# A job's scores, and its products of decayed scores and values, as single operations of a planner

## The chip, the cores and the metric

The kernel runs on one core of one Trainium2 chip. The time is device microseconds from start to end of an execution; the figure of a kernel is the median of its runs.

## What is computed

The reference is a gated linear-attention layer followed by two feed-forward layers, all in float32:

```
for t in range(768):                                  # 4 batches, 8 heads, head size 40
    m_new  = max(f_gate[t] + m, i_gate[t])
    f_stab = exp(f_gate[t] + m - m_new); i_stab = exp(i_gate[t] - m_new); m = m_new
    C = f_stab * C + i_stab * outer(v[t], k[t])
    n = f_stab * n + i_stab * k[t]
    y[t] = sigmoid(o_gate[t]) * (C @ q[t]) / max(abs(n . q[t]), 1)
x = y as 3072 tokens of 320
x = (h - tanh(h)) @ w_out,  h = x @ w_in              # 320 -> 2048 -> 320
x = g(h) @ w_out,  h = x @ w_in,  g(h) = h for h >= 1, 0 for h <= -1, (h + 1)^2 / 4 between
```

## The kernel before

The attention is done in chunks of 128 positions. A *job* is one chunk of one batch with its 8 heads; there are 24 jobs, numbered by chunk first and batch second. In a job the scores of each head (keys times queries, 128 by 128) are multiplied by a matrix of decays, and the product is multiplied with the values of the chunk. The earlier chunks enter through a state C that each job hands on to the next job of its batch.

On TensorE a job consists of these groups of matmuls, in the order of their priorities: the scores (`score`, line 465 in the profile; 8 matmuls, two at a time on two halves of the rows of the array, into two PSUM banks `t_s`), the products with the old state (line 503), the products of decayed scores and values (`pv`, line 509; 16 matmuls, two at a time on two halves of the columns of the array, into the bank `t_n`), the transposes of the result (line 532, `t_x`), and the new state (line 539, `t_c`). Each float32 matmul stands in the trace as two instructions, so a job has 16 of line 465 and 32 of line 509. VectorE makes the decays by a scan (line 453, tile `d`, a buffer for each half of the heads, three buffers in rotation) and multiplies the scores into them (line 471). Behind the products stand, in this order, ACT line 519 (the denominators, `dn`), VectorE lines 520 and 521, GpSimd line 522, VectorE line 526 (`x`), ACT line 529, and the transposes. The bank `t_n` is a single buffer. After the first two chunks the transposes of the gates (line 369, `t_i`; four of the six) use that same buffer.

The feed-forward layers run over 6 blocks of 512 tokens and 16 slices of 128 hidden units each, that is 96 steps per layer. A step has 8 matmuls for h (line 612; line 604 in the first steps) and 8 for the output (line 655; 12 in the second layer). The jobs of a block run during the feed-forward steps of the block before; the jobs of the first block run before any feed-forward step. In the first layer the weights are also converted on ACT and VectorE (lines 315 to 330).

The order on every engine is fixed ahead of time by a planner (`Plan`). Each operation has an engine, a cost in ns, a priority, and the buffers it reads and writes. On each engine the planner picks, among the operations that can start within 150 ns of the earliest one, that with the lowest priority number; ties go to the earlier start, then to the order in which they were stated. It counts 170 ns after a TensorE operation plus 60 ns until another engine may use the result, and 130 ns from another engine to TensorE. The instructions are then issued in that order, and each engine runs its own in order. Until the first feed-forward step the planner puts matmuls on zeros (line 755, `spare`) into the gaps that it foresees on TensorE.

Line 444 (`t_f`) spreads the decays of the first four jobs over the partitions by matmuls, and line 568 copies their transposed results for the first feed-forward steps.

Of the kernel before, what the change touches and what calls it, by code (L numbers as in the profile page):

```python
# [17 lines left out]
B, H, S, D = 4, 8, 768, 40  # L18
L = 128
# [5 lines left out]
E1 = D + 1  # L25
G3 = 3 * E1
HU = H // 2
# [45 lines left out]
class Plan:  # L73
# [20 lines left out]
    def op(self, eng, ns, prio, fn, r=(), w=(), out=None, lock=False):  # L94
        o = Op()
        o.eng, o.ns, o.prio, o.fn, o.seq, o.out = eng, ns, prio, fn, len(self.ops), out
        o.allocs, o.preds, o.succs = [], set(), []
        o.bufs, o.fill, o.lock = [], 0, lock
        key = lambda x: x if isinstance(x, tuple) else (x, None)

        for x in map(key, r):
            if x in self.last:
                o.preds.add(self.last[x])
            self.read.setdefault(x, []).append(o)
        for x in map(key, w):
            if x in self.last:
                o.preds.add(self.last[x])
            o.preds.update(self.read.pop(x, ()))
            self.last[x] = o
        o.preds.discard(o)  # L110
        for b in {key(x)[0] for x in (*r, *w)}:
            if isinstance(b, Buf):
                b.users.append(o)
                o.bufs.append(b)
        if any(b.place[0].startswith("late_") for b in o.bufs):
            o.preds.add(self.gate)
        self.ops.append(o)
        return o
# [102 lines left out]
def pe(n, m=128, wide=1):  # L221

    return max(wide * n / 2.4 + 13.5, m / 1.2 + 5)
# [3 lines left out]
def mlstm_moe_moe(ctx: ExitStack, tc: tile.TileContext, ig, fg, qk, q3, nat, w1, w2, cst, out):  # L227
    nc = tc.nc
# [25 lines left out]
    op = P.op  # L254
# [7 lines left out]
    def abuf(tag, shape, dtype, cap, name=None):  # L262
        att_tags.add(tag)
        return P.buf(of(ap), shape, dtype, tag, name or tag, cap)
# [128 lines left out]
    def jbank(n, what, name):  # L393

        tag = {"s0": "ta", "s1": "tb", "n": "tn", "x": "ta", "c": "tb", "f": "h"}[what]
        if n < FIRST and what in "s0s1xc":
            tag = (("ta", "tb"), ("a0", "a1"))[n % 2][what in ("s1", "x")]
        return bank(tag, name)
# [5 lines left out]
    def job(n, at, ld):  # L404

        c, b = divmod(n, B)
        last = c == NC - 1

        qt = abuf("qkraw", [64 + D, 1024], F32, 3)
# [25 lines left out]
        dk = {}  # L435
        d0 = wbuf(6 + n % 2, [128, 1024], F32, "d0") if n < FIRST else None
        wc = abuf("wc", [128, H], F32, 2)
        for u in range(2):
            p = at(0) if u == 0 else at(1)
# [8 lines left out]
            if d0 is None:  # L448
                d = abuf("d", [128, 512], F32, 3)
# [9 lines left out]

        sp = [jbank(n, f"s{u}", "t_s") for u in range(2)]  # L460

        def score(h):
            for u in range(2):
                t = qt[u * 64:u * 64 + D]
                nc.tensor.matmul(sp[u][:, h * L:(h + 1) * L], t[:, 512 + h * L:512 + (h + 1) * L],  # L465
                                 t[:, h * L:(h + 1) * L], start=True, stop=True)

        for h in range(HU):
            op("PE", 2 * pe(L, 128, 2), at(1), lambda h=h: score(h), [(qt, 0), (qt, 1)], [sp[0], sp[1]])
        for u in range(2):  # L470
            op("DVE", dve(512), at(2 + u), lambda p=sp[u], d=dk[u][0]: nc.vector.tensor_tensor(  # L471
                out=d(), in0=p.t, in1=d(), op=ALU.mult), [sp[u], dk[u][1]], [dk[u][1]])
# [2 lines left out]
        K, V, O = (nt, 0), (nt, 1), (nt, 2)  # L475
        v3 = lambda: nt[:, DM:DM + H * E1]
# [21 lines left out]
        p = jbank(n, "n", "t_n")  # L498
        parts = [(k, 120 if k < 2 else 80, G3 if k < 2 else 2 * E1) for k in range(3)]
        if c > 0:  # L500
            C = Cst[b, c]
            for k, r, w in parts:
                op("PE", 2 * pe(w, 128, 2), at(2.5), lambda k=k, r=r, w=w: nc.tensor.matmul(  # L503
                    p[:, k * G3:k * G3 + w], q[0:r, k, :], C[0:r, k * G3:k * G3 + w],
                    start=(k == 0), stop=False, skip_group_check=True), [(q, k // 2), C], [p])
        def pv(d, h):

            for z in (0, 64):
                nc.tensor.matmul(  # L509
                    p[z:z + 64, h * E1:(h + 1) * E1], d[:, z:z + 64], v3()[:, h * E1:(h + 1) * E1],  # L510
                    start=(c == 0 and h == 0), stop=(h == H - 1), skip_group_check=True)

        for u in range(2):
            for i in range(HU):
                h = u * HU + i
                op("PE", 125, at(4), lambda u=u, i=i, h=h: pv(dk[u][0]()[:, i * L:(i + 1) * L], h), [dk[u][1], V], [p])
        pn = lambda: p[:, 0:H * E1].rearrange("p (h e) -> p h e", e=E1)
        dn = abuf("dn", [128, H], F32, 1)
        op("ACT", 180, at(5), lambda: nc.scalar.activation(dn.t, pn()[:, :, D], AF.Abs), [p], [dn])
# [16 lines left out]
        if not last:  # L536
            pc = jbank(n, "c", "t_c")
            for k, r, w in parts:
                op("PE", 2 * pe(w, 120, 2), at(7), lambda k=k, r=r, w=w: nc.tensor.matmul(  # L539
                    pc[0:r, k * G3:k * G3 + w], nt[:, k * 120:k * 120 + r], v3()[:, k * G3:k * G3 + w],  # L540
                    start=True, stop=True), [K, V], [pc])
# [4 lines left out]
            for h in range(3):  # L546
                op("ACT", 330, at(8), lambda h=h: nc.scalar.activation(
                    y(to, h), y(pc, h), AF.Copy, scale=cs[0:120, C_HM + h:C_HM + h + 1]), [pc, "cs"], [to])
                if h < 2:
                    z = slice(2 * G3 + h * E1, 2 * G3 + (h + 1) * E1)  # L550
                    op("ACT", 280, at(8), lambda h=h, z=z: nc.scalar.activation(
                        to[0:80, z], pc[0:80, z], AF.Copy, scale=cs[0:80, C_HM + h:C_HM + h + 1]), [pc, "cs"], [to])
            if old is not None:
                for k, r, w in parts:
                    z = slice(k * G3, k * G3 + w)
# [10 lines left out]
        z = slice((n - BLK0[k]) * L, (n - BLK0[k] + 1) * L)  # L566
# [200 lines left out]
    def jobs(k):  # L767
        for i, (a, _) in enumerate(GROUPS):
            if i > 1 and a * B == BLK0[k]:
                gates(i, GATES[i])  # L770
                decays(i, DECAYS[i])
        for n in range(BLK0[k], BLK0[k] + BLK[k]):
            if k == 0:
                job(n, lambda s: JOB0 + JOBD * n + JOBS * s, LOAD[n])
            else:
                st = NF * (k - 1) + NF * (n - BLK0[k]) / BLK[k] - AHEAD
                job(n, lambda s: st + s, st - LOADS)
# [5 lines left out]
    for f in range(NF):  # L783
        p = W_CONV[f] if f < len(W_CONV) else f - W_AHEAD
# [102 lines left out]
```

## Time and profile before

| | us |
|---|---|
| median of 3 runs | 849.0 |
| lowest and highest run | 844.51 and 849.15 |
| the profiled execution | 847.22 |
| its span, first to last instruction | 845.4 |
| TensorE busy in the span | 831.9 |
| VectorE, ACT, GpSimd busy | 562.7, 417.0, 134.1 |

The profile shows one execution. The span leaves out 1.8 us that lie around it. A matmul's shown duration reaches beyond the start of the next one, since they overlap; what a group costs TensorE is read from its start to the start of the next row.

### The profile page before, as it was taken

To read this page: it belongs to the slowest core of one execution; us is meant where nothing else is said; L and a number is where in the kernel's file an instruction comes from. 1 tells how busy PE (TensorE), PEld (TensorE's weight loads), DVE (VectorE), ACT (ScalarE), POOL (GpSimd) and SP (SyncE) were. 2 spreads that over 40 slices of the span, in tenths; PEclk is the share of its full clock that TensorE was granted. 3 is DMA by queue.
4 is the path that set the end of the run, shared out by engine and by line. 5 is a ranking of instruction groups with operands and counts; after the bars stand their busy time and mean duration, and the time that the engine had idled before them with its cause. 6 is when DMAs were issued, how large, how long until landed. Compare 5 with 4: busy or idle time off the path is not lost.

```text
span 845.4 us, 13194 instructions
## 1 busy us (share of the span) xinstructions
PE 831.9 (98%) x5027; PEld 691.4 (82%) x5031; DVE 562.7 (67%) x920; ACT 417.0 (49%) x792; POOL 134.1 (16%) x170
## 2 busy tenths in 40 slices
PE   8999998999999999999999999999999999999997
PEld 6647766787888788878888889999999999999997
DVE  6998998888878756565446675565555655655554
ACT  3877755666665534433345553443443433433432
POOL 3231124322223321121003020020100100100000
PEclk9999999999999999999999999999999999999999
DMA  8974557566765432341145320020010000000000
GB/s 220 349 219 141 180 185 246 171 214 223 239 196 171 120 107 90 84 140 39 37 147 158 103 88 1 1 82 1 16 66 0 32 2 1 32 1 1 32 1 31
DMA packets 56515, 88.02 MB, mean 104 GB/s; under 512 B 4708, under 2 KB 37892, under 8 KB 56452
## 3 DMA queue, kind: packets, MB, share of 16 engines
q1 hardware_dynamic: 56404, 87.17, 32.8%
q8 instruction: 39, 0.64, 0.3%
q14 instruction: 24, 0.20, 0.1%
q10 hardware_dynamic: 48, 0.02, 0.0%
HBM read 72.59 MB, written 14.58 MB: 103 GB/s over the span
## 4 chain that ended last, share of the span: by engine, by line
PE 84%; DMA 0%; issue 0%; DVE 0%; DVEq 0%
PE h L612 39%; PE a L655 32%; PE t_o L655 5%; PE t_n L509 2%; PE t_s L465 2%; PE t_n L503 1%; PE t_c L539 1%; PE t_x L532 1%; DMA fb<-fr_d 0%; DVE C L556 0%; PE t_i L369 0%; DVE ob L700 0%; DVE x L526 0%; DVE d L453 0%; DVEq L453 0%
## 5 line engine op out<-in xcount | busy, mean ns | idle before, releaser
L612 PE MATMUL h<-x,w 128*128 128x512 f32 x1504 | 388.9, 397 | 1.9 <-ACT w L326 1.5
L612 PEld LDWEIGHTS h<-x,w 128*128 128x128 f32 x1504 | 275.1, 188 | 57.2 <-ACT w L326 2.8
L643 DVE TENSOR_TENSOR gl<-g,gh 128x512 fp32r<-128x512 f32 x188 | 134.1, 713 | 94.6 <-ACT gh L642 93.5
L642 ACT CAST gh<-g 128x512 fp32r<-128x512 f32 x188 | 116.6, 620 | 117.9 <-DVE g L639 72.8
L655 PE MATMUL a<-gh,w 128*128 128x512 f32 x460 | 150.8, 395 | 0.3 <-ACT gh L642 0.3
L637 ACT ACTIVATE g<-g,half 128x512 f32<-128x512 f32 x96 | 69.4, 723 | 121.1 <-DVE g L635 121.1
L655 PE MATMUL a<-w,gh 128*128 128x320 f32 x576 | 127.7, 308 | 0.0
L639 DVE TENSOR_TENSOR g<-h,g 128x512 f32<-128x512 f32 x96 | 66.3, 691 | 75.5 <-ACT g L637 75.5
L655 PE MATMUL a<-gl,w 128*128 128x512 f32 x276 | 107.1, 393 | 0.0
L655 PEld LDWEIGHTS a<-w,gh 128*128 128x128 f32 x576 | 100.2, 188 | 7.3
L630 ACT ACTIVATE g<-h 128x512 f32<-128x512 f32 x92 | 54.9, 597 | 92.7 <-PE h L612 92.5
L655 PEld LDWEIGHTS a<-gh,w 128*128 128x128 f32 x460 | 85.2, 188 | 18.2 <-ACT gh L642 0.8
L631 DVE TENSOR_TENSOR g<-h,g 128x512 f32<-128x512 f32 x92 | 63.2, 687 | 54.9 <-ACT g L630 54.1
L655 PE MATMUL a<-w,gl 128*128 128x320 f32 x288 | 88.9, 309 | 0.0
L635 DVE TENSOR_SCALAR g<-h 128x512 f32<-128x512 f32 x96 | 66.2, 690 | 8.0 <-PE h L612 8.0
L655 PEld LDWEIGHTS a<-gl,w 128*128 128x128 f32 x276 | 51.6, 188 | 11.1 <-DVE gl L643 0.2
L655 PEld LDWEIGHTS a<-w,gl 128*128 128x128 f32 x288 | 54.0, 188 | 0.0
L583 POOL TENSOR_TENSOR x<-xl,x 128x1024 fp32r<-128x1024 f32 x6 | 14.5, 2412 | 241.1 <-ACT x L582 241.1
L453 DVE TENSOR_TENSOR_SCAN d<-fb,scan_id 128x512 f32<-128x512 f32 x40 | 49.4, 1239 | 4.1 <-PE t_n L509 3.4
L522 POOL TENSOR_TENSOR nat<-nat,dn 128x320 f32<-128x320 f32 x24 | 29.1, 1213 | 99.3 <-DVE dn L521 96.7
L655 PE MATMUL t_o<-w,gh 128*128 128x320 f32 x192 | 43.9, 309 | 0.0
L471 DVE TENSOR_TENSOR d<-t_s,d 128x512 f32<-128x512 f32 x48 | 31.2, 680 | 10.9 <-PE t_s L465 9.1
(105 smaller groups left out, 825.2 us busy)
## 6 DMA issues: line engine op xcount, KB each, us to landing
w<-in_w_dram SPq DMA_DIRECT2D x32, 703.6 KB
nat<-in_nat_dram SPq DMA_DIRECT2D x24, 484.0 KB
fb<-fr_d SPq DMA_DIRECT2D x40, 256.0 KB
qkraw<-in_qk_dram SPq DMA_DIRECT2D x48, 160.0 KB
w_d<-w SPq DMA_DIRECT2D x16, 352.0 KB
w<-w_d SPq DMA_DIRECT2D x16, 352.0 KB
xr_d<-xo SPq DMA_DIRECT2D x18, 256.0 KB
q<-in_q_dram SPq DMA_DIRECT2D x20, 180.0 KB
```

What stands on the lines that cost most here:

```text
L453: op("DVE", dve(1024), p, lambda o=dk[u][0], i=f[u][0]: nc.vector.tensor_tensor_scan(out=o(), data0=i(), data1=scan_id, initial=0.0, op0=A ...
L471: op("DVE", dve(512), at(2 + u), lambda p=sp[u], d=dk[u][0]: nc.vector.tensor_tensor(out=d(), in0=p.t, in1=d(), op=ALU.mult), [sp[u], dk[u ...
L522: op("POOL", pool(DM), at(5), lambda: nc.gpsimd.tensor_tensor(out=o3().rearrange("p (h e) -> p h e", e=D), in0=o3().rearrange("p (h e) -> ...
L612: op("PE", pe(n), prio, lambda i=i, c=c, s=s: nc.tensor.matmul(p[:, :n], w[:, c:c + 128], x[:, s, :n], start=(i == 0), stop=(i == 7)), [(w ...
L630: op("ACT", act(n), prio + 0.5 - FFN, lambda: nc.scalar.activation(t[:, :n], p[:, :n], AF.Tanh), [p], [t])
L631: op("DVE", dve(n), prio + 0.5 - FFN, lambda: nc.vector.tensor_tensor(out=t[:, :n], in0=p[:, :n], in1=t[:, :n], op=ALU.subtract), [p, t], [t])
L635: op("DVE", dve(n), prio + 0.5 - FFN, lambda: nc.vector.tensor_scalar(t[:, :n], p[:, :n], -1.0, 1.0, op0=ALU.max, op1=ALU.min), [p], [t])
L637: op("ACT", act(n, 1), prio + 0.5 - FFN, lambda: nc.scalar.activation(t[:, :n], t[:, :n], AF.Square, bias=half[:, 0:1], scale=0.5), [t, "h ...
L639: op("DVE", dve(n), prio + 0.5 - FFN, lambda: nc.vector.tensor_tensor(out=t[:, :n], in0=p[:, :n], in1=t[:, :n], op=ALU.max), [p, t], [t])
L642: op("ACT", act(n), prio + 1 - FFN, lambda: nc.scalar.copy(gh[:, :n], t[:, :n]), [t], [gh])
L643: low = lambda e: e.tensor_tensor(out=gl[:, :n], in0=t[:, :n], in1=gh[:, :n].bitcast(F32), op=ALU.subtract)
L655: mm = lambda o, a, b, start, stop, r, cost: op("PE", cost, prio, lambda: nc.tensor.matmul(o(), a(), b(), start=start, stop=stop), r[0], r[1])
```

## The change

The four operations for a job's scores become one operation with the same eight matmuls in the same order, and its planned cost goes from 4 times 240 ns to 1088 ns. The eight operations for a job's products of decayed scores and values (one for each head, each depending on the decays of its own half of the heads) become one operation with the same sixteen matmuls in the same order; it depends on both halves, and its planned cost goes from 8 times 125 ns to 1128 ns.

```diff
-        def score(h):
-            for u in range(2):
-                t = qt[u * 64:u * 64 + D]
-                nc.tensor.matmul(sp[u][:, h * L:(h + 1) * L], t[:, 512 + h * L:512 + (h + 1) * L],
-                                 t[:, h * L:(h + 1) * L], start=True, stop=True)
-
-        for h in range(HU):
-            op("PE", 2 * pe(L, 128, 2), at(1), lambda h=h: score(h), [(qt, 0), (qt, 1)], [sp[0], sp[1]])
+        def scores():
+            for h in range(HU):
+                for u in range(2):
+                    t = qt[u * 64:u * 64 + D]
+                    nc.tensor.matmul(sp[u][:, h * L:(h + 1) * L], t[:, 512 + h * L:512 + (h + 1) * L],
+                                     t[:, h * L:(h + 1) * L], start=True, stop=True)
+
+
+        op("PE", 200 + 2 * HU * 111, at(1), scores, [(qt, 0), (qt, 1)], [sp[0], sp[1]])
...
-        def pv(d, h):
-
-            for z in (0, 64):
-                nc.tensor.matmul(
-                    p[z:z + 64, h * E1:(h + 1) * E1], d[:, z:z + 64], v3()[:, h * E1:(h + 1) * E1],
-                    start=(c == 0 and h == 0), stop=(h == H - 1), skip_group_check=True)
-
-        for u in range(2):
-            for i in range(HU):
-                h = u * HU + i
-                op("PE", 125, at(4), lambda u=u, i=i, h=h: pv(dk[u][0]()[:, i * L:(i + 1) * L], h), [dk[u][1], V], [p])
+        def pv():
+
+            for h in range(H):
+                d = dk[h // HU][0]()
+                for z in (0, 64):
+                    t = h % HU * L + z
+                    nc.tensor.matmul(
+                        p[z:z + 64, h * E1:(h + 1) * E1], d[:, t:t + 64], v3()[:, h * E1:(h + 1) * E1],
+                        start=(c == 0 and h == 0), stop=(h == H - 1), skip_group_check=True)
+
+        op("PE", 200 + 2 * H * 58, at(4), pv, [dk[0][1], dk[1][1], V], [p])
```

## Rows read from the trace of the kernel before

**Rows 1.** The page, parts 1 and 2: busy time of the engines, granted clock in tenths.
```profile
PE 831.9 (98%) x5027; PEld 691.4 (82%) x5031; DVE 562.7 (67%) x920; ACT 417.0 (49%) x792; POOL 134.1 (16%) x170
PEclk9999999999999999999999999999999999999999
```

**Rows 2.** Windows: stretch, its length, busy us per engine, clock, DMA share, GB/s.
```profile
41.00:128.60 87.60, 84.54 (x489) 57.39 (x489) 79.69 (x134) 61.01 (x118) 20.14 (x32) 1.00 0.59 181
...
131.60:135.60 4.00, 3.99 (x16) 2.95 (x16) 3.32 (x6) 1.30 (x4) 2.01 (x2) 0.57 0.68 233
135.60:380.00 244.40, 244.18 (x1639) 196.94 (x1640) 179.86 (x314) 132.87 (x296) 62.27 (x86) 1.00 0.52 166
```

**Rows 3.** Groups of TensorE instructions by line: count, busy us, mean ns, idle before.
```profile
L509 PE MATMUL t_n<-nat,d 128*64 128x41 f32 x768 | 31.1, 233 | 0.2 <-issue 0.2
```

**Rows 4.** Timeline of TensorE, job 20: start us, us, engine, line, instruction, count.
```profile
362.58 1.43 PE L612 MATMUL h<-x,w 128*128 128x512 f32 x5
363.94 0.67 PE L509 MATMUL t_n<-nat,d 128*64 128x41 f32 x16
364.53 0.50 PE L612 MATMUL h<-x,w 128*128 128x512 f32 x1
364.97 0.67 PE L509 MATMUL t_n<-nat,d 128*64 128x41 f32 x16
365.56 0.73 PE L612 MATMUL h<-x,w 128*128 128x512 f32 x2
366.14 0.62 PE L655 MATMUL a<-gh,w 128*128 128x512 f32 x2
```

**Rows 5.** Timeline of TensorE, job 21, from its scores on.
```profile
377.85 1.16 PE L465 MATMUL t_s<-qkraw 40*128 40x128 f32 x16
378.94 0.73 PE L612 MATMUL h<-x,w 128*128 128x512 f32 x2
379.51 0.62 PE L655 MATMUL a<-gh,w 128*128 128x512 f32 x2
379.97 0.40 PE L655 MATMUL a<-gl,w 128*128 128x512 f32 x1
...
381.43 1.13 PE L509 MATMUL t_n<-nat,d 128*64 128x41 f32 x32
382.50 2.12 PE L612 MATMUL h<-x,w 128*128 128x512 f32 x8
384.45 0.62 PE L655 MATMUL a<-gh,w 128*128 128x512 f32 x2
```

**Rows 6.** Timeline of TensorE: first halves of the products of jobs 5 and 7.
```profile
76.14 0.67 PE L509 MATMUL t_n<-nat,d 128*64 128x41 f32 x16
...
125.62 0.67 PE L509 MATMUL t_n<-nat,d 128*64 128x41 f32 x16
```

**Rows 7.** Timeline of TensorE: second half of the scores of job 1.
```profile
13.98 0.72 PE L465 MATMUL t_s<-qkraw 40*128 40x128 f32 x8
```

**Rows 8.** Timeline of TensorE and ACT, job 3 to the first feed-forward step.
```profile
35.16 0.67 PE L509 MATMUL t_n<-nat,d 128*64 128x41 f32 x16
...
40.94 4.95 PE L604 MATMUL h<-xf,wf 128*128 128x512 f32 x10
...
35.94 0.18 ACT L519 ACTIVATE dn<-t_n 128x8 f32<-128x8 f32 x1 [0.81 <-PE t_n L509]
...
39.58 0.25 ACT L529 COPY x<-x 128x64 f32<-128x64 f32 x1
```

**Rows 9.** Timeline of TensorE: transposes of the gates of chunks 2 and 3.
```profile
131.61 0.21 PE L369 MATMUL t_i<-cs,ig 32*128 32x32 f32 x1 [2.81 <-DVE x L526]
...
199.63 0.24 PE L369 MATMUL t_i<-cs,ig 32*128 32x32 f32 x1
```

**Rows 10.** Timeline of VectorE ahead of that first transpose.
```profile
128.94 1.43 DVE L453 TENSOR_TENSOR_SCAN d<-fb,scan_id 128x512 f32<-128x512 f32 x1 [0.23 <-DMA fb<-fr_d]
...
130.98 0.48 DVE L526 TENSOR_TENSOR x<-t_n,nat 128x320 f32<-128x320 f32 x1
```

## The prediction, made before the result

> **What bounds the kernel now.** I read the page first. TensorE is busy in 831.9 of 845.4 us and VectorE in 562.7, at full granted clock in nearly every slice [rows 1], so time that TensorE spends on a job's small matmuls is time of the kernel wherever TensorE has no idle time. The windows by stage say where that is: from 135.6 to 380.0 us TensorE is busy 244.18 of 244.40 us; from 41.0 to 128.6 us VectorE is busy 79.69 of 87.60 us and TensorE has 3.06 us idle [rows 2]. In the first stretch a gain on TensorE counts in full, in the second it may only become a wait. The groups by line then give the changed work its size: line 509 has 768 instructions, 32 for each of 24 jobs [rows 3]. Last I went through the timeline of TensorE job by job, to see which groups are broken up already.
>
> **The scores.** Their sixteen instructions stand in one piece in 23 of the 24 jobs, as in job 21, where they take 1.09 us from 377.85 to 378.94 [rows 5]. Only job 1 has them in two pieces of eight, the second at 13.98 us [rows 7], before any feed-forward work. So I cost this half of the edit at nothing after the head. What hides it is that all four operations become ready together and share one priority. If something still slipped in between in the new plan, it could not split a single operation, so the edit cannot add a switch here.
>
> **The products.** In 14 jobs (5, 7 and 9 to 20) they stand in two pieces of 16: in job 5 the first starts at 76.14 us, in job 7 at 125.62 us [rows 6], and in job 20, the last of them, at 363.94 us [rows 4]. Job 20 shows why: the second half needs the second half of the decays, and while the planner waits for it, a lone matmul of line 612 is put in. That is what the change forbids. Jobs 4, 6, 8 and 21 to 23 are in one piece before the change, so both forms can be priced.
>
> Split form, job 20, from the first row behind its scores: 362.58 to 366.14 us, 3.56 us for 32 small instructions and 8 feed-forward matmuls (5, 1 and 2) [rows 4]. Whole form, job 21, also from behind its scores: 378.94 to 384.45 us, 5.51 us for 32 small ones and 18 feed-forward matmuls (2, then 8 of line 655, then 8) [rows 5]. A plain feed-forward matmul costs 0.23 us (379.51 to 379.97 us for two [rows 5]). Ten of them are 2.30 us, which leaves 3.21 us for the whole form with 8. The difference is 0.35 us for each split that goes. It is made of the way out of the small matmuls and back in: in the whole form 32 take 381.43 to 382.50, 1.07 us; in the split form the halves take 0.59 us each, and the lone matmul between them takes 0.44 us in place of 0.23 us [rows 4, 5].
>
> Twelve of the 14 splits (jobs 9 to 20) lie after 135.6 us, where TensorE has no idle time: 12 times 0.35 is **4.2 us less**. Jobs 5 and 7 lie where VectorE is the fuller engine; I count nothing for them, 0.7 us at most.
>
> **What it costs in the head.** There the two halves of job 3 are apart; the second half starts at 35.16 us and the first feed-forward step at 40.94 us [rows 8]. With one operation, all 32 start when the second half's decays are there. TensorE only fills its time with matmuls on zeros here, so its own work is free, but the result is ready 1.07 minus 0.59, some 0.5 us later. Line 519 on ACT already waits 0.81 us for it at 35.94 us, and ACT runs in order, through the conversions queued behind it to line 529 at 39.58 us, which the transposes need [rows 8]. So the 0.5 us is on the path. Job 1's second scores group takes 13.98 to 14.62 us, and moving it ahead of the spreading of decays beside it adds between 0 and 0.65 us. I take **0.5 us more** for the head, with 0 and 1.15 as ends; 0.5 because the wait of line 519 is seen, and the other is not.
>
> **What else moves.** The planned cost of a job rises by 127 ns for the scores (1088 against 961) and 128 ns for the products (1128 against 1000), and it now fits the measured 1.09 and 1.07 us. The planner therefore lays out the whole order again. Its net effect on TensorE's order elsewhere I take as nothing; the ends are the one large pause that the trace has, gone, or more like it. The added wait, for the second half of the decays, holds nothing behind it on TensorE that the planner can't place ahead: there are feed-forward matmuls at either side of every job after the first four. The buffer of the first half's decays is released later, by at most the 0.59 us of a half and the 0.44 us of the lone matmul; VectorE's next scan waits for that, and VectorE has 64 us free in the 244 us of the long stretch [rows 2].
>
> Sum: 4.2 less, 0.5 more, **3.7 us less** than the profiled execution, 847.2 us: 843.5 us. The median of the three runs lies 1.8 us above that execution and the lowest 2.7 us below it. I put the median to come at **844 us**.
>
> **Rivals.** *The pause goes too.* Before the transposes of the gates at 131.61 us TensorE is idle for 2.81 us [rows 9], and the next 4.0 us have a mean clock of 0.57, that is mostly the lower of the two levels, 1.2 GHz [rows 2], which loses 0.43 of 4.0, 1.7 us. Together 4.5 us. The pause comes from VectorE's order: line 526, which frees the bank, runs at 130.98 us behind a scan that began at 128.94 us after waiting for a DMA [rows 10]. A new plan may order these otherwise. Then 839.5 us. For it: job 7's products are split right before it, so this place is laid out anew. Against it: the DMA isn't touched.
>
> *The gain is eaten.* The splits go, but the new order puts 3 to 4 us of small waits into the stretch before 135 us, or the lone matmuls' place turns into waits: 848 us, no change. For it: that stretch already loses 3 us, and VectorE has little room there. Against it: the long stretch lies after it and can't give its gain back, having so little idle time to begin with.
>
> *Slower, by new pauses.* Three more gate transposes, after the one with the pause, share the single bank with the products, and the products now hold it until both halves are done. At 199.63 us the first of the three starts without a wait [rows 9]; if its place in the order comes before line 526 is done, it stops all of TensorE, at 4.5 us a time. The point from which it decides is all three pausing: 13.5 less 3.7, 857 us. Against it: the planner counts the bank's release, and this one runs free now.
>
> *The clock.* The clock here is at its upper level through the whole stretch from 135.6 us on, and through jobs with whole products as well as with split ones [rows 1, 2]. If longer runs of small matmuls pulled it down, 20 jobs at 1.7 us would be 34 us, 878 us. The Trainium skill (TensorE: Matmul & The Clock Gate, Part 4: PE-mode transpose) says that transposes do not count as busy for the clock in the way that other matmuls do; read for small matmuls too, that would speak against the change, and by that rule the clock would fall at each job. The trace disagrees with such a reading: jobs 21 to 23 are whole, and the slices that hold them show full clock [rows 1].
>
> **How the numbers follow.** The forecast, splits gone and little else, gets 0.52; the pause gone too 0.20; the gain eaten 0.18; slower by new pauses 0.09; the clock 0.01. The likeliest gives 844. The range reaches down to the pause gone with the largest saving (839.5 less 0.7 for jobs 5 and 7 and 0.5 for the head, 838.3) and up to the highest run of before with the head's upper end (849.15 plus 1.15): **838 to 850.5**. The last two rivals stay outside. One per cent, 8.5 us, is about what a measurement of this kernel tells from no change. Faster by more needs 840.5 or less: most of the pause case and a little of the forecast, 0.19. Slower by more is 0.09. Within it, 0.72.
>
> **What would show it.** Right: line 509 in 24 pieces of 32 in the timeline, 1.07 us each, with no lone matmul inside; line 465 in 24 pieces of 16; the stretch from job 9 to the end of job 23 shorter by some 4 us; first feed-forward step near 41.4 us. Whether the pause is kept is read at the third gate transposes and in the clock of the microseconds behind them. Wrong: pieces of 32 and no shorter stretch, which would mean that the switch price moved to the neighbours; or idle time ahead of lines 369, 503 or 612 that was not there.

## The result, and the profile after

| | before | after |
|---|---|---|
| median us | 848.02 (4 runs, 844.51 to 849.15) | 838.14 (4 runs, 837.77 to 841.14) |
| ratio of the times | 1 | 0.9898, 95% interval 0.986 to 0.9937 |
| profiled execution us | 847.22 | 838.19 |
| its span us | 845.4 | 836.4 |

The change is faster by 1.0%. A second comparison, with more runs of the kernel before (run e5 below), gives 0.9926, interval 0.9905 to 0.9947; that ratio is 6.3 us, and the medians differ by 7.0 us. What belongs to the change is nearer to that second comparison, as the experiments show; the first pair of profiles differs by 9.0 us.

Busy time of the kernel after, from its page, against [rows 1]; and its products, against [rows 3]:

```profile
PE 824.7 (99%) x5029; PEld 688.9 (82%) x5029; DVE 564.0 (67%) x920; ACT 417.9 (50%) x792; POOL 137.9 (16%) x170
```

```profile
L513 PE MATMUL t_n<-nat,d 128*64 128x41 f32 x768 | 27.2, 231 | 0.0
```

TensorE is busy 7.2 us less with the same work, the matmuls on zeros of the start aside; line 509, now 513, shows 27.2 us in place of 31.1. All 24 jobs have their 32 instructions in one piece. To see where the 9.0 us went I cut both spans at the same work: first feed-forward step, last product of job 7, of job 8, of job 20, of job 23. The windows of the kernel before, with the columns of [rows 2]:

```profile
40.94:127.05 86.11, 83.05 (x480) 56.27 (x481) 78.23 (x131) 60.19 (x113) 19.56 (x31) 1.00 0.59 182
127.05:138.84 11.79, 8.98 (x82) 6.80 (x79) 9.73 (x19) 6.16 (x17) 5.95 (x8) 0.86 0.73 248
138.84:365.40 226.56, 226.38 (x1515) 182.39 (x1512) 168.99 (x296) 125.38 (x280) 58.07 (x81) 1.00 0.52 165
365.40:418.96 53.56, 53.41 (x364) 43.37 (x361) 29.86 (x51) 18.94 (x39) 6.77 (x8) 1.00 0.22 67
```

The same windows of the kernel after:

```profile
36.94:122.27 85.33, 82.27 (x479) 56.07 (x480) 79.78 (x134) 60.55 (x113) 22.41 (x31) 1.00 0.60 183
122.27:135.12 12.85, 10.11 (x88) 7.76 (x85) 10.51 (x21) 6.80 (x18) 5.80 (x8) 0.87 0.81 257
135.12:357.52 222.40, 221.95 (x1514) 181.19 (x1509) 168.61 (x293) 126.08 (x280) 59.36 (x81) 1.00 0.53 166
357.52:410.78 53.26, 53.10 (x363) 42.97 (x359) 30.21 (x51) 18.58 (x38) 6.72 (x8) 1.00 0.22 67
```

The first number behind each window is its length. From job 8 to job 20, where the twelve splits were, it falls from 226.56 to 222.40, 4.2 us. From the first feed-forward step to job 8 it is 98.18 after against 97.90 before. The end, behind job 23, falls from 426.5 to 425.6, all of it behind TensorE's last matmul.

The windows end at the same products, but they do not hold quite the same feed-forward work, since the new plan places some of it earlier. Counted in the two traces, the feed-forward matmuls go from 249 to 254 between the first step and job 8, from 749 to 746 between job 8 and job 20, and from 186 to 184 behind it. At 0.23 us each, some 0.7 of the 4.2 us are three matmuls that left the long stretch; 0.3 us of longer waits stand against that. So twelve splits were worth some 3.7 us, about 0.31 us each. And the stretch ahead of job 8, 0.3 us longer with 1.15 us more of these matmuls in it, became some 0.9 us cheaper for the same work: 0.1 to 0.2 us of that is shorter waits, and the rest, 0.7 us, is of the size of two splits, those of jobs 5 and 7. From the first feed-forward step to TensorE's last matmul all windows together are 4.2 us shorter.

And the head ends at 36.94 instead of 40.94, 4.0 us, where I had forecast 0.5 us more.

Job 20 in the timeline of the kernel after, against [rows 4]:

```profile
353.48 1.16 PE L466 MATMUL t_s<-qkraw 40*128 40x128 f32 x16
354.57 2.11 PE L613 MATMUL h<-x,w 128*128 128x512 f32 x8
356.62 1.13 PE L513 MATMUL t_n<-nat,d 128*64 128x41 f32 x32
357.68 0.73 PE L656 MATMUL a<-gh,w 128*128 128x512 f32 x2
358.25 0.39 PE L656 MATMUL a<-gl,w 128*128 128x512 f32 x1
```

From 354.57 to 358.25 there are 10 feed-forward matmuls and the products, 3.68 us; less two matmuls of 0.23 us that is 3.22 us, where [rows 4] had 3.56 us for the same work. The pause is still there, against [rows 9]:

```profile
126.73 0.21 PE L369 MATMUL t_i<-cs,ig 32*128 32x32 f32 x1 [2.74 <-DVE x L527]
```

### The profile page after: what moved, and what is told of

It is laid out like the page before. It is cut to its first block, busy times and chain, and to the rows that moved or that the text cites. A ratio compares the mean times of both kernels' runs of the same rounds, so it can differ in the third digit from the quotient of the medians.

```text
span 836.4 us, 13195 instructions
## 1 busy us (share of the span) xinstructions
PE 824.7 (99%) x5029; PEld 688.9 (82%) x5029; DVE 564.0 (67%) x920; ACT 417.9 (50%) x792; POOL 137.9 (16%) x170
## 4 chain that ended last, share of the span: by engine, by line
PE 84%; ACT 1%; DMA 1%; issue 0%; DVE 0%; DVEq 0%
PE h L613 39%; PE a L656 33%; PE t_o L656 5%; PE t_s L466 2%; PE t_n L513 2%; PE t_n L504 1%; PE t_c L540 1%; PE t_x L533 1%; DMA fb<-fr_d 1%; ACT L364 0%; ACT t_c L548 0%; ACT w L315 0%; DVE C L557 0%; PE t_i L369 0%; ACT t_c L552 0%
## 5 line engine op out<-in xcount | busy, mean ns | idle before, releaser
L613 PE MATMUL h<-x,w 128*128 128x512 f32 x1504 | 383.3, 395 | 1.5 <-ACT w L326 1.1
```

The costliest lines, as they stand in the source:

```text
L613: op("PE", pe(n), prio, lambda i=i, c=c, s=s: nc.tensor.matmul(p[:, :n], w[:, c:c + 128], x[:, s, :n], start=(i == 0), stop=(i == 7)), [(w ...
```

## The experiments

My theory after the result: the splits carry 4.2 us in the long stretch, some 2 us of the head come from the new order, and the rest of the first comparison is chance at the start. Rivals: the whole operations of the first four jobs bring 4 us each time, or the planned costs make the gain. Every ratio is against runs of the kernel before on the same chip, taken together with the run: their median is 847.05 us for e1 to e4, 846.57 for e5 to e8, 848.19 for e9 to e11 and 846.40 for e12. Medians compare within such a group; between groups it is the ratios that compare.

| run | what | median us | ratio, 95% interval | job 8 to job 20, us |
|---|---|---|---|---|
| e1 | before, again | 846.78 | 0.9999 (0.9983 to 1.0015) | 226.4 |
| e2 | whole in jobs 0 to 3 | 844.40 | 0.9978 (0.9961 to 0.9994) | 226.6 |
| e3 | whole from job 4 on | 841.23 | 0.9941 (0.9919 to 0.9964) | 222.5 |
| e4 | costs alone | 846.14 | 0.9990 (0.9970 to 1.0010) | 227.7 |
| e5 | after, again | 839.57 | 0.9926 (0.9905 to 0.9947) | 222.4 |
| e6 | products alone | 841.91 | 0.9952 (0.9937 to 0.9967) | 224.3 |
| e7 | scores alone | 845.99 | 0.9996 (0.9981 to 1.0011) | 226.9 |
| e8 | after, 12 splits put back | 843.71 | 0.9967 (0.9951 to 0.9984) | 226.5 |
| e9 | after, old costs | 840.61 | 0.9918 (0.9886 to 0.9951) | 223.1 |
| e10 | after, 6 slices on GpSimd | 837.05 | 0.9869 (0.9845 to 0.9893) | 222.4 |
| e11 | after, 11 slices on GpSimd | 837.72 | 0.9880 (0.9854 to 0.9906) | 222.3 |
| e12 | e10, scans behind x | 834.36 | 0.9846 (0.9818 to 0.9874) | 222.7 |

**e1, the kernel before once more.** No edit.

> The kernel before, once more, for its first 40 us. Theory (chance at the start): the changed kernel reached its first feed-forward step 4.0 us earlier (36.94 against 40.94 us), and 2.3 us of that stand already at the second ACT sigmoid (11.69 against 13.97 us), which waits for a load issued at the same moment in both; so another profile of the kernel before should show that sigmoid anywhere from 11.5 to 14 us and its first feed-forward step between 38.6 and 41 us. Rival (order): the sigmoid at 14 us and the first step at 40.9 us again, within 0.3 us. Time: no difference from the kernel before under either.

The second sigmoid began at 12.67 us, between the two, and the first feed-forward step at 40.03 us. So the start moves from run to run, as the theory had it. Whether chance is all of it, the next pair shows.

**e5, the kernel after once more.** No edit.

> The changed kernel once more, as the base of the runs beside it. Theory so far (the gain is 4.2 us in the long stretch, some 2 us in the head by order, and the rest chance of the clock and of the first loads): 7 to 8 us faster than the kernel before, about 839 us, and 7.6 us where runs of the same mean clock are compared. Rival (all of the 9.9 us of the first comparison belong to the change): 838.1 us again.

7.0 us by the medians and 6.3 by the ratio, so the theory's 7 to 8 at its lower end; the rival's 838.1 did not come again. In this profile the second sigmoid waits for its load just as long as in e1, which makes a fair pair; both have a mean clock of 0.998. On ACT, first e1, then e5:

```profile
12.67 0.47 ACT L482 ACTIVATE nat<-nat 128x320 f32<-128x320 f32 x1 [1.34 <-DMA nat<-in_nat_dram]
```

```profile
12.55 0.47 ACT L483 ACTIVATE nat<-nat 128x320 f32<-128x320 f32 x1 [1.32 <-DMA nat<-in_nat_dram]
```

And VectorE in e1, products, scans, denominators and x of the first jobs:

```profile
13.26 0.69 DVE L471 TENSOR_TENSOR d<-t_s,d 128x512 f32<-128x512 f32 x1 [0.47 <-ACT wc L456]
13.87 1.21 DVE L453 TENSOR_TENSOR_SCAN d<-t_f,scan_id 128x512 f32<-128x512 f32 x1
15.93 0.59 DVE L520 TENSOR_SCALAR dn<-dn 128x8 f32<-128x8 f32 x1 [0.84 <-ACT dn L519]
...
18.34 0.48 DVE L526 TENSOR_TENSOR x<-t_n,nat 128x320 f32<-128x320 f32 x1
...
37.09 0.49 DVE L526 TENSOR_TENSOR x<-t_n,nat 128x320 f32<-128x320 f32 x1 [0.61 <-POOL nat L522]
```

In e5:

```profile
13.14 0.69 DVE L472 TENSOR_TENSOR d<-t_s,d 128x512 f32<-128x512 f32 x1 [0.45 <-ACT wc L456]
13.75 2.33 DVE L453 TENSOR_TENSOR_SCAN d<-t_f,scan_id 128x512 f32<-128x512 f32 x2
15.99 0.24 DVE L521 TENSOR_SCALAR dn<-dn 128x8 f32<-128x8 f32 x1
...
17.54 0.48 DVE L527 TENSOR_TENSOR x<-t_n,nat 128x320 f32<-128x320 f32 x1
...
35.77 0.49 DVE L527 TENSOR_TENSOR x<-t_n,nat 128x320 f32<-128x320 f32 x1 [0.84 <-POOL nat L523]
```

In e1 VectorE does one scan and then waits 0.84 us for the denominators of job 0; in e5 the new plan puts job 1's second scan there, and there is no wait. Job 0's x comes 0.8 us sooner (18.34, 17.54), job 3's x 1.3 us sooner (37.09, 35.77). The last part lies behind x. TensorE in e1, the second half of job 3's products to the first step:

```profile
34.24 0.67 PE L509 MATMUL t_n<-nat,d 128*64 128x41 f32 x16
...
38.52 0.78 PE L532 MATMUL t_x<-cs,x 128*128 128x128 f32 x3
...
40.03 2.61 PE L604 MATMUL h<-xf,wf 128*128 128x512 f32 x5
```

In e5:

```profile
31.84 1.13 PE L513 MATMUL t_n<-nat,d 128*64 128x41 f32 x32
...
36.31 0.60 PE L533 MATMUL t_x<-cs,x 128*128 128x128 f32 x3 [0.21 <-DVE x L527]
...
37.65 4.52 PE L605 MATMUL h<-xf,wf 128*128 128x512 f32 x9
```

From x's start to the first step it takes 2.94 us in e1 and 1.88 us in e5. The difference, 1.06 us, is ACT's order. The last of the three transposes needs the copy of line 529, first e1, then e5:

```profile
38.67 0.25 ACT L529 COPY x<-x 128x64 f32<-128x64 f32 x1
```

```profile
36.29 0.24 ACT L530 COPY x<-x 128x64 f32<-128x64 f32 x1 [0.34 <-DVE x L527]
```

x ends at 37.58 us in e1 and at 36.26 us in e5. In e1 the copy stands behind two conversions of weights and starts 1.09 us after x; in e5 the plan has ACT idle for x, and the copy starts 0.03 us after it. From the copy's start to the first step it is 1.36 us in both. In all, from the first scores to the first step, 32.7 us became 30.4 us: 2.3 us by order. The other profiles agree: with the old head this stretch takes 33.4 us (the first profile of the kernel before) and 33.3 us (e3), with the new one 30.0 to 30.6 us (the first profile after, e2, e8). The remaining 1.7 us of the first pair's 4.0 are 0.8 us before the first scores (7.59 against 6.81 us, same instructions) and some 0.9 us of the later load in the kernel before (its sigmoid began at 13.97 us).

**e2, whole operations in the first four jobs alone.** The condition decides which form a job gets:

```
+        whole = n < FIRST
+        if whole:
+            ... scores, pv as after
+        else:
+            ... score, pv as before
```

> Scores and products are single operations in the first four jobs alone; the plan still splits the products of jobs 5, 7 and 9 to 20. Theory (splits in the long stretch carry 4.2 us, the head only the 1.7 us that are left of 4.0 beside the chance at the start): 1 to 2.5 us faster than the kernel before, about 846 us. Rival (the whole operations of the first four jobs bring the head's 4 us each time): 4 to 5 us faster, about 843.5 us.

2.65 us by the medians, just above the theory's figure, 1.9 us by the ratio, within it; the rival's 4 to 5 us did not come. The long stretch stayed at 226.6 us.

**e3, whole operations from job 4 on.** `whole = n >= FIRST`.

> Scores and products are single operations from job 4 on alone; the first four jobs are as before. Theory: the 12 splits that lie in the stretch where TensorE has no idle time are gone, 12 times 0.35 us: 4.2 us faster than the kernel before, about 843.8 us, and in the profile the stretch from the scores of job 8 to the end of job 23's products is 4 us shorter. Rival (the new planned costs or the head made the gain): under 2 us faster.

The stretch from job 8 to job 20, TensorE's busy time second behind the window:

```profile
137.80:360.30 222.50, 222.05 (x1513) 181.11 (x1509) 167.70 (x294) 125.67 (x280) 59.37 (x81) 1.00 0.53 168
```

222.5 us, all of the change's gain there, with the head as before (first step at 41.39 us). The time fell by 5.8 us, the ratio says 5.0; 4.2 was expected. Some 0.8 us of the gain lie behind TensorE's last matmul, which the 4.2 does not hold (see the open part at the end of the next section).

**e4, the planned costs alone.**

```
-            op("PE", 2 * pe(L, 128, 2), at(1), lambda h=h: score(h), ...
+            op("PE", 272, at(1), lambda h=h: score(h), ...
-                op("PE", 125, at(4), lambda u=u, i=i, h=h: pv(...
+                op("PE", 141, at(4), lambda u=u, i=i, h=h: pv(...
```

> Nothing is made whole; only the planned costs rise as in the change (four times 272 ns for the scores, eight times 141 ns for the products). The plan splits the products of 11 jobs after the first four (8, 10, 12 to 20), 11 of them in the long stretch against 12 before. Theory: the price of a split decides, so at most 0.4 us faster in the long stretch and no measurable difference in time, within 2 us of the kernel before. Rival (the better planned costs make the gain): 4 us faster or more.

No difference that can be measured. The costs without the whole operations bring nothing that shows.

**e6, the products alone; e7, the scores alone.** Each takes one of the two hunks of the diff.

> Only the products are single operations; the scores are four operations as before. Theory: the products alone carry the stretch (4.2 us) and most of the head, so 6 to 8 us faster than the kernel before, within 1 us of the whole change. Rival (the scores' part carries the head): 4 to 5 us faster.

> Only the scores are single operations; the plan splits the products of 16 jobs after the first four (5 to 20), two more than before, one of them in the long stretch. Theory: no gain, 0 to 1 us slower than the kernel before by two splits of 0.35 us, 847 to 848 us. Rival (the scores carry the head): 2 us faster.

The scores alone bring no difference that can be measured, though in e7's profile the head is 31.6 us, 1.1 us shorter than e1's; two more splits, which that plan makes, cost some 0.6 us against it. The products alone bring 4.7 us by the medians and 4.1 by the ratio, at the rival's size, not the 6 to 8 I expected, though the rival's reason is wrong: the head is as good as in e5 (30.7 us from first scores to first step). What is missing is in the long stretch, 224.3 instead of 222.4 us, where TensorE now waits 0.63 us ahead of line 512 and 0.17 us ahead of a job's scores (a third wait, 0.43 us, stands in e5 too), and which holds two feed-forward matmuls more, 0.46 us. The last 0.7 us there stay open.

**e8, the splits put back into the new plan.** When jobs 9 to 20 are issued, the next TensorE operation goes between the two halves:

```
+            if o in self.halves:
+                o.fn(0)
+                rest = o
+                continue
             o.fn()
+            if rest is not None and o.eng == "PE":
+                rest.fn(1)
+                rest = None
```

> The plan of the changed kernel, order kept, but when jobs 9 to 20 are issued the next TensorE operation of the plan is put between the two halves of the products: twelve splits are back and nothing else moves. Theory (a split costs 0.35 us of TensorE): 4.2 us slower than the changed kernel of the same call, about 843 us. Rival (the splits cost little and the new order makes the gain): within 1 us of the changed kernel.

Job 20 in its timeline:

```profile
358.17 2.11 PE L624 MATMUL h<-x,w 128*128 128x512 f32 x8
360.21 0.67 PE L522 MATMUL t_n<-nat,d 128*64 128x41 f32 x16
360.81 0.49 PE L667 MATMUL a<-gh,w 128*128 128x512 f32 x1
361.23 0.67 PE L522 MATMUL t_n<-nat,d 128*64 128x41 f32 x16
361.83 0.50 PE L667 MATMUL a<-gh,w 128*128 128x512 f32 x1
362.17 0.40 PE L667 MATMUL a<-gl,w 128*128 128x512 f32 x1
```

4.00 us from 358.17 to 362.17 for the 10 matmuls and the products that took 3.68 us in the kernel after. The window from job 8 to job 20:

```profile
135.20:361.70 226.50, 226.05 (x1514) 182.32 (x1510) 168.66 (x296) 125.11 (x279) 58.53 (x80) 1.00 0.52 163
```

226.5 us against 222.4 in e5, and 4.1 us by the medians (843.71, 839.57). One matmul more lies in e8's window, the one put between job 20's halves, so 3.9 us are the splits: 0.32 us each, as in job 20. This decides the main point: with the order of all other work kept, twelve splits cost what the long stretch had gained.

**e9, whole operations at the old costs.** `8 * pe(L, 128, 2)` and 1000 in place of 1088 and 1128.

> The changed kernel with the planned costs of before (961 and 1000 ns for the two whole operations). Theory (a whole operation, not its planned cost, makes the gain): the long stretch 4 us shorter and the head 2 us shorter as in the change, 839 to 841 us, within 2 us of the changed kernel. Rival (half of the gain is the new costs, since with the scores in four pieces of the old cost the gain was only 4.7 us): 842 us.

Within the theory's range: 840.61 us. The long stretch takes 223.1 us against e5's 222.4; TensorE waits 0.40 us at 151.75 us for the products' decays, as in e6 at the same place. From the first step to TensorE's last matmul e9's profile takes 0.9 us more than e5's. So costs that fit the measured time may be worth about 1 us once the operations are whole; the times do not show it, since e9's ratio, 0.9918, is no worse than e5's 0.9926.

**e10 and e11, less work for VectorE ahead of the pause.** For a given set of slices of the first layer, the low part of the weights is made on GpSimd:

```
-            vec(prio, y - x, part, [u, (w, 0)], [(w, 1)])
+            vec(prio, y - x, part, [u, (w, 0)], [(w, 1)],
+                eng="POOL" if layer == 0 and f in (5, 7, 9, 11, 13, 15) else "DVE")   # e11: f > 4
```

> The changed kernel with the low part of the weights of six slices of the first layer (5, 7, 9, 11, 13, 15; line 330) made on GpSimd in place of VectorE, 0.95 us each. Theory (from 41 to 127 us VectorE sets the time, which is why the splits of jobs 5 and 7 brought nothing there): VectorE has 5.7 us less to do in that stretch and the pause of 2.7 us ahead of the gate transposes shrinks or goes; 2 to 5 us faster than the changed kernel, 835 to 838 us. Rival (the stretch is set by the chain of job 7 and its loads, or GpSimd's longer operations stand in VectorE's way): no faster, 839 to 843 us.

> The same for all eleven slices from 5 on. Theory: 10 us less on VectorE, of which no more than the waits of the stretch can come back (2.7 us pause, 2.5 us of smaller waits, 1.7 us of clock): 3 to 7 us faster than the changed kernel, 832 to 836 us. Rival: TensorE waits for the weights from GpSimd instead, which takes about 2 us for what VectorE does in 0.95; 840 us or slower.

e10 is faster than e5: its ratio's interval ends at 0.9893, and e5's begins at 0.9905. The size is less sure, 2.5 us by the medians of two groups and 4.8 us by the ratios. The pause shrank to 1.75 us:

```profile
124.16 0.21 PE L370 MATMUL t_i<-cs,ig 32*128 32x32 f32 x1 [1.75 <-DVE x L528]
```

In return TensorE now waits 1.71 us at 107.64 us, ahead of line 614, for weights on ACT; all its waits behind the first step together fall from 6.35 us in e5 to 4.33 us.

e11 misses its figure: the pause is gone, but TensorE waits 1.24 us at 108.87 and 2.22 us at 113.89 us instead, for weights and activations on ACT. Giving GpSimd more than some of the slices turns one wait into others.

**e12, the order ahead of x.** VectorE in e10, what stands ahead of x of job 7 (line 528):

```profile
120.13 2.78 DVE L454 TENSOR_TENSOR_SCAN d<-fb,scan_id 128x512 f32<-128x512 f32 x2
122.84 0.77 DVE L558 SCALAR_TENSOR_TENSOR C<-C,gw,t_c 120x123 f32<-120x123 f32 x3
123.53 0.48 DVE L528 TENSOR_TENSOR x<-t_n,nat 128x320 f32<-128x320 f32 x1
```

The edit, on e10 (`done[n]` is the operation that makes x):

```
+            if n == 8:
+                scan.preds.add(done[7])
```

> The kernel with six slices on GpSimd (run e10), and the scans of job 8 wait in the plan for line 526's operation of job 7 (x, the last on VectorE before the transposes that TensorE stops for). In run e10 two scans, 2.78 us, stood ahead of it and TensorE stopped for 1.75 us. Theory (VectorE's order ahead of x makes the pause): the pause falls under 1 us, and with it most of the microseconds at half clock that followed it; 1 to 4 us faster than run e10, 833 to 836 us. Rival (the weights' conversions that take the scans' place, 1.8 us, keep the pause, or job 8 comes later by as much): 837 us, no difference from run e10.

VectorE and then TensorE in e12:

```profile
121.60 0.48 DVE L531 TENSOR_TENSOR x<-t_n,nat 128x320 f32<-128x320 f32 x1
```

```profile
122.22 0.21 PE L370 MATMUL t_i<-cs,ig 32*128 32x32 f32 x1 [0.89 <-DVE x L531]
```

As the theory had it, the pause is 0.89 us, half of e10's, and in the 10.2 us from its end on the mean clock is 0.83 instead of 0.67 in these two profiles; what is left of the pause is not explained. 834.36 us is the lowest median here, 0.9846 of the kernel before (interval 0.9818 to 0.9874). By the medians that is 2.7 us less than e10; but the two were measured on different chips, and the intervals of their ratios overlap, so the shorter pause is shown, and a gain over e10 beyond the noise is not.

## Why the prediction came out as it did

The direction was right; the forecast of 844 was 6 us too high. That 838.14 still lies in the range of 838 to 850.5 is luck: the range's lower end was worked out as 838.3, from a rival that did not occur, and rounded down. The same kernel's second median, 839.57, is inside with more room.

**The scores: right.** Nothing by themselves (e7).

**The products: right in mechanism, and in the sum partly by compensation.** The fourteen splits behind the first step became none, and so did those of the first four jobs. 0.35 us each was read from two jobs; job 20 gives 0.34, the splits put back give 0.32 in job 20 and 3.9 us in all (e8). I counted twelve at 0.35, 4.2 us. From the first step to TensorE's last matmul the gain is 4.2 us in the first pair and 4.3 us between e1 and e5: fourteen splits at 0.32 are 4.5 us, and TensorE's waits there are 0.2 us longer. The Trainium skill (TensorEngine Tiling (Array Packing), Key Properties) says that a change of the tiling mode drains TensorE; it gives no price for it. The rows fit that: a split is two more such changes, and e8 shows their price with the order of all other work kept. That the drain makes up the whole of that price, no run here shows.

**Jobs 5 and 7: at the upper end.** I counted nothing for them and 0.7 us at most, because VectorE is the fuller engine there (79.78 of 85.33 us). But the window up to job 7 is 0.8 us shorter, and by the count above some 0.7 us is of the size of these two splits. No run put them back alone.

**The head: wrong, and it is the step that failed.** I put 0.5 us more, with ends 0 and 1.15; the runs show 2.3 us less at equal arrival of the load. The step assumed that all 32 instructions start when the second half's decays are there. They do not: the single operation exists in the planner alone. In the kernel after, the products of job 3 begin at 31.14 us while VectorE makes that half from 30.62 to 31.31 us, and only its own instructions wait for it. And I took the planner's new layout as neutral, when the head is where the order on VectorE and ACT sets the time: one scan placed into a wait of 0.84 us on VectorE, and the copy of line 529 that starts right behind x on ACT. I had named that chain, through the conversions to line 529, but took the order on it as fixed. Ends of 0 and 1.15 excluded a gain without a reason.

**The base: off by 0.65 us.** A forecast of 844 with 3.7 us less means a base of 847.7; with 26 runs the kernel before has a median of 847.05 us. Of the first comparison's 9.9 us by the medians about 7 come again; e5's span is 7.4 us shorter than e1's, 2.4 of it in the head, 4.3 from the first step to TensorE's last matmul, and 0.75 behind that. Of the 5.9 us between forecast and time the head is 2.8, the base 0.65 and the end 0.75 to 0.9; the rest, 1.5 us, is about what lies between the two medians of the kernel after, 838.14 and 839.57.

**The pause: kept, as the forecast's own case had it.** Its cause, VectorE's order ahead of line 526, was argued; e12 shows it for half of the pause that e10 has. The rival's time of 839.5 is met only because the head gave as much. **The clock rival** did not occur: the two windows from job 8 to job 23 show 1.00. **New pauses** did not occur: ahead of the later gate transposes TensorE does not wait. One wait of 0.45 us, ahead of a job's scores at 202.70 us, is new.

One part stays open. From the start of the last copy the kernel before takes 4.5 and 4.4 us to the end of its span, in its two profiles, and the kernel after and all others 3.7 us, e4 with its costs alone too; the outputs are written in the same order. The DMA packets show a difference. In both profiles of the kernel before, and in no other, a packet of 8192 bytes of the instruction queue runs there among the last packets of the output, for 0.49 and 0.42 us; DMA queues of the kernel before from 840.89 to 845.50 us:

```profile
q14 instruction: 1, 0.01, 0.7%
```

The last output packet then ends 3.25 and 3.13 us behind the start of that copy, in place of 2.5 us. So about 0.8 of the 7 us do not come of the splits or of the head. That this packet is the cause is argued; no run was made on it.

## What to carry to other kernels

A group of small matmuls that uses half of the array's rows or columns should stay in one piece: here each way out to full-size matmuls and back costs 0.32 to 0.34 us, and in a stretch where TensorE never idles all of it counts. A planner that is told of many small operations can split them where some of them are ready late, as this one did in 14 jobs of the last 20; make the unit of planning the group, and give it the group's measured cost. When an edit changes what a planner sees, its largest effect can lie where another engine sets the time, so bound that in both directions, and compare repeated profiles at equal arrival of the first loads before believing a difference at the start. Two windows that end at the same row can still hold different work: count it before reading their lengths.

## What the runs showed of the hardware that I had not expected

The same pause is followed by very different stretches at the lower clock. The windows behind it, 10.2 us each, in e3 (pause 2.74 us), the kernel after (2.74 us) and e2 (2.81 us); the seventh number behind each window is the granted clock:

```profile
131.00:141.20 10.20, 10.20 (x86) 8.14 (x87) 9.49 (x18) 5.42 (x12) 4.59 (x6) 1.00 1.00 332
```

```profile
126.70:136.90 10.20, 10.17 (x79) 8.03 (x80) 8.41 (x17) 4.40 (x11) 4.61 (x6) 0.83 0.99 333
```

```profile
128.60:138.80 10.20, 10.12 (x67) 8.04 (x67) 5.76 (x10) 2.74 (x6) 3.88 (x5) 0.51 0.96 303
```

In the first the clock does not fall, in the third it stays at 1.2 GHz nearly throughout, after nearly the same work and idle time. The kernel after and e3 have the same order of work around the pause. This goes with most of the spread of this kernel's times: of the 26 runs of the kernel before, the two with a mean clock of 1.000 have a median span of 843.0 us, nine with 0.998 843.9, twelve with 0.996 845.8 and two with 0.994 847.5. At 0.998 the kernel after has spans of 836.3 to 837.1 us, again some 7 us less.
